# Attention's q, k and v laid out by the host, with fp32 products in place of split fp16 ones

## The chip, the cores and the metric

The program runs on one core of a Trainium2 chip. The metric is device time in microseconds (us) of one execution, lower is better. The figure for the kernel before is the median of three runs; the trace is of one execution more.

## The reference

Three layers follow each other. Attention over B=4 batches, H=8 heads, S=576 tokens and D=64 has a mask that leaves each query at most 32 keys: heads 0 to 3 see the 32 last tokens, heads 4 to 7 every fourth of the 128 last. Its output feeds two mixtures of experts, one with a greedy assignment of 288 tokens to each of 8 experts, one dense with balanced weights.

```python
def _attn_ref(q, k, v):                       # 4, 8, 576, 64
    scores = scale * np.matmul(q, k.transpose(0, 1, 3, 2))
    rel = pos[:, None] - pos[None, :]
    mask_plain = (rel >= 0) & (rel < 32)
    mask_dil = (rel >= 0) & (rel < 32 * 4) & (rel % 4 == 0)
    masks = np.stack([mask_plain if h < H // 2 else mask_dil for h in range(H)], axis=0)
    scores = np.where(masks[None, :, :, :], scores, -1000000000.0)
    scores = scores - np.max(scores, axis=-1, keepdims=True)
    attn = np.exp(scores)
    attn = attn / (np.sum(attn, axis=-1, keepdims=True) + 1e-09)
    return np.matmul(attn, v).astype(np.float32)

def _moe_ref(x, w_gate, w1, w2):              # x 2304 x 512, 8 experts, 1024 hidden
    order = np.argsort(-(x @ w_gate).flatten())
    # in this order each token goes to the first expert that still has room (288 each)
    for e in range(E):
        h = np.maximum(x[assigned == e] @ w1[e], 0.0)
        out[assigned == e] = h @ w2[e]

def _moe2_ref(x, w_gate, w1, w2):             # every expert on every token
    P = np.exp(logits - logits.max())
    for _ in range(8):
        P /= P.sum(1, keepdims=True) + 1e-09
        P /= P.sum(0, keepdims=True) + 1e-09
        P *= N / E
    for e in range(E):
        out += P[:, e:e + 1] * (np.maximum(x @ w1[e], 0.0) @ w2[e])
```

## The kernel before

Products are made of fp16 halves: an fp32 operand a is stored as a high part (fp16 of a) and a low part (fp16 of the rest), and a product is the sum of high·high, high·low and low·high, three matrix products into one accumulator.

**Attention, preparation.** q and k come in with tokens on partitions, in five tiles of 64 or 128 partitions (`TILES`, `load_qk`). Each tile is copied and scaled (`t_copy`: k on VectorE, q on ScalarE), transposed in fp32 on TensorE (`t_group`), and taken out of PSUM as a high part by ScalarE and a low part by VectorE (`t_evac`). `warm` are idle products of zeros.

**Attention, the loop.** A unit is 96 queries of up to eight heads: four of the plain kind (kind 0) and four of the dilated kind (kind 1), whose tokens are taken in residue order so that its window is 32 wide too; kind 1 runs one block ahead. There are NU = 25 units, and only the 128 keys that a block can see take part. Iteration n works on several units at once, in program order on each engine:

```python
scores(n); row_max(n)                  # mask products (L215) and products q·k (L223); L230, L231
p_evac(n - 1, p_trans(n - 1))          # transposes of the probabilities (L247); L255, L256
exps(n)                                # eight exponentials on ScalarE (L239)
pv(n - 2, ...)                         # L269 to L271, and logits of finished tokens
v_split(n + 1); load_v(n + 3)          # L198 on VectorE, L200 and L201 on GpSimd; L118
x_out(n - 3)                           # xo on ScalarE (L288), the rest on GpSimd, store on SyncE (L293)
```

The two heads of a pair lie in opposite halves of the partitions (rows 0 to 63 and 64 to 127), and the products of a pair follow each other on TensorE. The mask is an additive bias: two products of an identity with a table (`mk`, which GpSimd's DMA queue brings) open the accumulation. `x_out` writes a unit's output, as high and low part, to the array `xd` in device memory, from a tile `xo` that comes from a pool of two buffers in units 0 to 17; later units have buffers of their own, in tiles of the preparation that are free by then.

**After attention.** Greedy routing (from the logits) runs on VectorE, GpSimd and TensorE. The experts of the first mixture gather their tokens from `xd` (`gather_x`, L781) and their weights (`fetch_gather`, L772; the weights are fp32 and converted by ScalarE, L751) by indirect DMA on GpSimd's queue. Products of the first mixture are L800, of the second L1064 and L1102; its balancing (L1207) are small fp32 products. `fetched(ph)` starts phase ph's fetches; each `next(w)` issues two weight gathers.

Every engine runs its instructions in program order, and every DMA is issued by the engine that it is written for: SyncE (SP), ScalarE or GpSimd (POOL).

Of the kernel before, what the change touches and what calls it, by code (L numbers as in the profile page):

```python
# [23 lines left out]
QB = 96  # L24
NJ = S // QB
NI = S // 4
SQ = 2.0 ** 7
# [5 lines left out]
SC = 0.125 / (SQ * SQ)  # L33
# [50 lines left out]
TILES = [(0, 64), (64, 128), (192, 128), (320, 128), (448, 128)]  # L84
FILL = {0: 4}
TURN = {NU - 1: (NU - 7, NU - 6), NU: (NU - 5, NU - 4), NU + 2: (NU - 2, NU - 1)}


def attention(tc, q, k, v, masks, wg, ident, xd, L, zero):

    nc = tc.nc
    with ExitStack() as ctx:
# [6 lines left out]
        raw, RP, VR, VS, SS, PP, PT, XT = {}, {}, {}, {}, {}, {}, {}, {}  # L99
        src = {"q": q, "k": k}  # L100
        T = {nm: one.tile([128, 2, 4, B * S], F16, name="t" + nm) for nm in "kq"}

        def load_qk(t, nm):
            f0, n = TILES[t]
            x = raw[t, nm] = ld.tile([128, H, 4, D], F32, name="raw" + nm)
            f = f0
            while f < f0 + n:
                b, i = divmod(f, NI)
                m = min(NI - i, f0 + n - f)
                nc.sync.dma_start(x[f - f0:f - f0 + m].rearrange("i h r d -> i h (r d)"),  # L110
                                  src[nm][b].rearrange("h (i r) d -> i h (r d)", r=4)[i:i + m])
                f += m

        def load_v(u):
            t = VR[u] = vp.tile([128, H, D], F32, name="rawv")
            for kind, (b, j) in UNITS[u].items():
                for p, n, tok, st in tokens_of(max(QB * j - 32, 0), 128, kind):
                    nc.sync.dma_start(t[p:p + n, 4 * kind:4 * kind + 4], bass.AP(  # L118
                        tensor=v.tensor, offset=v.offset + (b * H + 4 * kind) * S * D + tok * D,
                        ap=[[st * D, n], [S * D, 4], [1, D]]))  # L120
# [8 lines left out]
        idh = one.tile([QB, QB], F16)  # L129
        mk = one.tile([QB, MASKS.shape[1], 2, 128], BF)  # L130
# [3 lines left out]
        c128 = one.tile([128, D], F32)  # L134
# [7 lines left out]
        nc.gpsimd.memset(c128, SQ)  # L142
# [6 lines left out]
        def t_copy(t, nm, eng):  # L149
            n = TILES[t][1]  # L150
            x = RP[t, nm] = ld.tile([128, 4, H, D], F32, name="rp" + nm)
            o, i = x[:n], raw.pop((t, nm))[:n].rearrange("i h r d -> i r h d")
            if eng is nc.scalar:
                nc.scalar.activation(o, i, AF.Copy, scale=SQ)
            else:
                nc.vector.tensor_scalar(o, i, SQ, None, op0=OP.mult)

        GC = [0]

        def t_group(t, nm, kind):  # L160
            f0, n = TILES[t]
            x = RP[t, nm]
            tag, bufs = (("ps_s", 2), ("ps_p", 1), ("ps_s", 2))[GC[0] % 3]
            GC[0] += 1
            p = ps.tile([128, 2, 512], F32, name=tag, bufs=bufs)
            for a in range(2):
                for r in range(4):
                    h = 4 * kind + 2 * a
                    nc.tensor.transpose(p[:, a, r * n:(r + 1) * n], x[:n, r, h:h + 2, :], idf[:n, :n])
            return p  # L170

        def t_evac(t, nm, kind, p):
            f0, n = TILES[t]
            pi = p[:, :, :4 * n].rearrange("p a (r i) -> p a r i", r=4)
            if kind == 0:
                parts = [(0, n, [T[nm][:, x, 0:2, 4 * f0:4 * (f0 + n)].rearrange("p a (i r) -> p a r i", r=4)
# [499 lines left out]
class Moe:  # L676
# [540 lines left out]
    def stage1(self, ctx):  # L1217
# [183 lines left out]
```

## Time and profile before

| | |
|---|---|
| median of three runs | 1892.06 us (1890.17 to 1892.47) |
| the profiled execution | 1893.46 us |
| its span (first to last record) | 1891.7 us |
| TensorE busy | 1784.1 us (94% of the span) |
| VectorE busy | 1413.5 us (75%) |
| ScalarE busy | 895.5 us (47%) |
| GpSimd busy | 285.8 us (15%) |

Busy shares are means over stages with different limits: the greater part of the span is the two mixtures of experts, and attention is its start. A stage is read from its own stretch of the span. The profiled execution is 1.40 us above the median.

### The profile page before, as it was taken

How to read it: one execution, taken by the hardware profiler on the slowest of the kernel's cores; microseconds unless marked ns; L12 is line 12 of the kernel's file. 1: busy time of each engine (PE TensorE's matmuls, PEld its weight loads, DVE VectorE, ACT ScalarE, POOL GpSimd, SP SyncE). 2: the span in 40 equal slices, each digit the busy share in tenths (PEclk: the TensorE clock that was granted, in tenths of full speed). 3: DMA queues.
4: the chain of work that ended last, by engine and by line, in shares of the span. 5: the costliest groups of instructions: out<-in, count | busy, mean ns of one | idle time of the engine just before them, and what ended most of it. 6: DMA issues, size and time to landing. Idle time of an engine off the chain costs nothing.

```text
span 1891.7 us, 36726 instructions
## 1 busy us (share of the span) xinstructions
PE 1784.1 (94%) x15082; PEld 1315.0 (70%) x15082; DVE 1413.5 (75%) x2681; ACT 895.5 (47%) x1558; POOL 285.8 (15%) x359
## 2 busy tenths in 40 slices
PE   6898589899999999999999999999999999999998
PEld 4676366666667665677777777777777777777776
DVE  5996687667764477777888788788878878887665
ACT  6885233334334335554555444455544445554333
POOL 0583322223323000000000000000000000000111
PEclk7997699999999999999999999999999999999999
DMA  9275543345445241243533334443333444333120
GB/s 226 66 154 149 113 100 79 108 96 115 115 92 136 73 153 69 82 162 144 193 134 116 141 148 162 154 184 138 120 138 143 162 163 174 141 119 136 75 93 35
DMA packets 139817, 241.21 MB, mean 128 GB/s; under 512 B 74208, under 2 KB 107232, under 8 KB 132736
## 3 DMA queue, kind: packets, MB, share of 16 engines
q1 hardware_dynamic: 118384, 151.25, 24.7%
q0 software_dynamic: 20592, 87.53, 15.6%
q8 instruction: 118, 1.93, 0.4%
q14 instruction: 51, 0.42, 0.1%
q10 hardware_dynamic: 672, 0.08, 0.0%
HBM read 173.74 MB, written 61.74 MB: 124 GB/s over the span
## 4 chain that ended last, share of the span: by engine, by line
PE 58%; issue 10%; DVE 6%; ACT 3%; POOL 1%; DMA 1%; POOLq 0%; ACTq 0%; SPq 0%; DVEq 0%
PE mm L1064 25%; PE mm L1102 22%; PE mm L800 6%; PE mm L881 4%; DVE hl L1021 1%; DMA raw<-in_w2a_dram,widx 1%; POOL out_dram L1116 1%; DVE r L936 1%; ACT raw L933 1%; PE mm L837 1%; DVE w1l L752 1%; ACT acc L1126 0%; PE r L552 0%; DMA lst<-idx 0%; ACT hh L1020 0%
## 5 line engine op out<-in xcount | busy, mean ns | idle before, releaser
L1064 PE MATMUL mm<-xb,w1h 128*128 128x384 f16 x2352 | 575.8, 327 | 5.0 <-DVE mm L1035 4.7
L1102 PE MATMUL mm<-w2h,hh 128*128 128x256 f16 x1764 | 480.8, 273 | 7.5 <-DVE t L1132 4.0
L1102 PE MATMUL mm<-w2h,hl 128*128 128x256 f16 x1764 | 480.8, 273 | 0.0
L1102 PE MATMUL mm<-w2l,hh 128*128 128x256 f16 x1764 | 480.8, 273 | 0.0
L1064 PE MATMUL mm<-xb,w1l 128*128 128x384 f16 x1176 | 384.7, 327 | 0.0
L1102 PEld LDWEIGHTS <-hh 128*128 128x128 f16 x3528 | 345.2, 98 | 51.6 <-issue 9.6
L1064 PEld LDWEIGHTS <-w1h 128*128 128x128 f16 x2352 | 230.7, 98 | 160.1 <-issue 12.7
L1102 PEld LDWEIGHTS <-hl 128*128 128x128 f16 x1764 | 172.6, 98 | 20.0
L1021 DVE TENSOR_TENSOR hl<-r,hh 128x1536 f16<-128x1536 f32 x84 | 147.5, 1756 | 41.3 <-ACT hh L1020 41.3
L1064 PEld LDWEIGHTS <-w1l 128*128 128x128 f16 x1176 | 115.4, 98 | 76.8 <-issue 1.2
L982 POOL DMA_DIRECT2D ws<-raw x48 | 26.0, 541 | 941.6 <-ACT raw L933 674.1
L1016 ACT ACTIVATE r<-mm 128x384 f32<-128x384 f32 x252 | 119.1, 481 | 98.4 <-PE mm L1064 98.3
L1020 ACT ACTIVATE hh<-r 128x1536 f16<-128x1536 f32 x84 | 124.6, 1483 | 46.1 <-DVE r L1045 44.2
L1027 ACT ACTIVATE mm<-mm 128x384 f32<-128x384 f32 x84 | 40.3, 480 | 181.4 <-PE mm L1064 181.4
L1021 DVE TENSOR_TENSOR hl<-S,hh 128x1152 f16<-128x1152 f32 x84 | 113.5, 1351 | 0.0
L800 PE MATMUL mm<-xt,w1h 128*128 128x288 f16 x512 | 97.6, 290 | 6.6 <-ACT xt L814 6.6
L1112 DVE SCALAR_TENSOR_TENSOR acc<-t,P,acc 128x512 f32<-128x512 f32 x126 | 94.7, 752 | 4.5
L803 ACT ACTIVATE w1h<-mm 128x288 f16<-128x288 f32 (+1 forms) x120 | 46.9, 397 | 107.5 <-PE mm L800 98.8
L1020 ACT ACTIVATE hh<-S 128x1152 f16<-128x1152 f32 x84 | 96.3, 1147 | 0.0
L933 ACT ACTIVATE raw<-raw 128x1024 f16<-128x1024 f32 x48 | 50.6, 1055 | 96.3 <-DVE raw L918 50.1
L804 DVE SCALAR_TENSOR_TENSOR w1l<-mm,w1h 128x288 f16<-128x288 f32 (+1 forms) x120 | 50.5, 435 | 57.0 <-ACT w1h L803 56.1
L800 PE MATMUL mm<-x2l,w0h 128*128 128x256 f16 x288 | 80.4, 279 | 9.0 <-DVE x2l L842 7.3
(288 smaller groups left out, 3294.2 us busy)
## 6 DMA issues: line engine op xcount, KB each, us to landing
xb<-xw SPq DMA_DIRECT2D x30, 1344.0 KB
ws<-raw POOLq DMA_DIRECT2D x48, 448.0 KB
ws<-r POOLq DMA_DIRECT2D x48, 448.0 KB
raw<-in_w2b_dram SPq DMA_DIRECT2D x32, 512.0 KB
raw<-in_w1b_dram SPq DMA_DIRECT2D x56, 256.0 KB
w1h<-ws SPq DMA_DIRECT2D x6, 1792.0 KB
w1l<-ws SPq DMA_DIRECT2D x6, 1792.0 KB
w2h<-ws SPq DMA_DIRECT2D x6, 1792.0 KB
```

What stands on the lines that cost most here:

```text
L800: nc.tensor.matmul(p, a[:, k, 128 * f:128 * (f + 1)], rhs(k, b), start=(k == 0 and i == 0), stop=(k == KT - 1 and i == 2))
L803: nc.scalar.activation(h[0][:, f, :n], p, AF.Relu)
L804: nc.vector.scalar_tensor_tensor(h[1][:, f, :n], p, 0.0, h[0][:, f, :n], op0=OP.max, op1=OP.subtract)
L881: nc.tensor.matmul(p, a[:, f, c], b[:, f, :], start=(f == 0 and n == 0), stop=(f == FT - 1 and n == 2))
L933: self.nc.scalar.activation(hi[:, k], x, AF.Copy, scale=sw)
L1016: nc.scalar.activation(o, p, AF.Relu, scale=SH)
L1020: yield nc.scalar.activation(hq[0][:, i, k], x, AF.Copy)
L1021: yield V.tensor_sub(hq[1][:, i, k], x, hq[0][:, i, k])
L1027: nc.scalar.activation(Q[i], P[i], AF.Copy)
L1064: nc.tensor.matmul(p, w[u][:, 2 * j + i // 2, k, 128 * (i % 2):128 * (i % 2 + 1)], x[:, v, r, j], start=(q in (1, 5) and j == 0 and n == 0 ...
L1102: nc.tensor.matmul(p, h[u][:, i, a, 128 * t:128 * (t + 1)], w[v][:, i, b, :], start=(q in (1, 7) and i == 0 and j == 0), stop=(q in (2, 3) ...
L1112: V.scalar_tensor_tensor(self.acc[:, r, :], x, self.P[:, r, e:e + 1], self.acc[:, r, :], op0=OP.mult, op1=OP.add)
```

## The change

The host lays out q and k with the 64 elements of a head on partitions (two heads of a pair one above the other, 128 partitions) and the tokens along the free axis, the dilated kind in residue order; and v as, for each block and kind, the 128 tokens on partitions with a column of 1/256 beside each head's 64. On the chip the preparation goes away: a unit's operands are slices of what was loaded, in fp32. A score takes one fp32 product a head in place of three fp16 ones, and so does the product with v. q and k are loaded in 16 loads (each one batch and kind, 128 partitions of 1152 elements), v in 8 (128 partitions of 1560 elements). Stores to `xd` from units 18 to 24 and the tiles of the turned x have own buffers. In `fetched`, all four weight gathers of the first expert come ahead of its gather of tokens.

```diff
+def lay_qk(a):
+    a = a.reshape(B, 4, 2, S, D).transpose(0, 2, 4, 1, 3).reshape(B, 128, 4, S)
+    r = a[:, :, 2:].reshape(B, 128, 2, NI, 4).swapaxes(3, 4).reshape(B, 128, 2, S)
+    return np.concatenate([a[:, :, :2], r], 2)
+def lay_v(a):
+    out = np.full((B, 2, 128, NJ, 4, D + 1), 1.0 / SX, np.float32)
+    for kind in range(2):
+        for j in range(NJ):
+            for p, n, tok, st in tokens_of(max(QB * j - 32, 0), 128, kind):
+                x = a[:, 4 * kind:4 * kind + 4, tok:tok + st * (n - 1) + 1:st]
+                out[:, kind, p:p + n, j, :, :D] = x.transpose(0, 2, 1, 3)
+    return out
...
+        def load_qk(nm, b, kind):
+            x = raw[nm, b, kind] = one.tile([128, 2, S], F32, name="raw%s%d%d" % (nm, kind, b))
+            nc.sync.dma_start(x, src[nm][b, :, 2 * kind:2 * kind + 2])
+        def load_v(b, kind):
+            x = VR[b, kind] = vp.tile([128, NJ, 4, D + 1], F32, name="rawv%d" % kind, bufs=2)
+            nc.sync.dma_start(x, v[b, kind])
...
-        load_qk(0, "k")
-        nc.scalar.dma_start(idf, ident)
-        load_qk(0, "q")
-        for nm in "kq":
-            load_qk(1, nm)
+        for kind in (1, 0):
+            for nm in "kq":
+                load_qk(nm, 0, kind)
+            if kind:
+                nc.scalar.dma_start(idf, ident)
+        load_v(0, 1)
+        load_v(0, 0)
         nc.gpsimd.dma_start(mk, masks)
...
-        def t_copy(t, nm, eng):
...
-        def t_group(t, nm, kind):
...
-        def t_evac(t, nm, kind, p):
...
-        def v_split(u):
...
             for g in range(gs.start, gs.stop):
-                for n, (x, y) in enumerate(((0, 0), (0, 1), (1, 0))):
-                    for s in range(2):
...
+                for s in range(2):
+                    h = 2 * g + s
+                    b, j = kinds[g // 2]
+                    nc.tensor.matmul(p[:, s, g, :], op_ap("q", h, b, j), op_ap("k", h, b, j), start=False,
+                                     stop=(g + 1 == gs.stop), skip_group_check=True)
...
-            nc.vector.tensor_scalar(nm[:, :, gs], nm[:, :, gs], -SC, None, op0=OP.mult)
+            nc.vector.tensor_mul(nm[:, :, gs], nm[:, :, gs], negc[:, :, gs])
...
-            nc.scalar.activation(th[:, :, gs], pp[:, :, gs], AF.Copy)
-            nc.vector.tensor_sub(tl[:, :, gs], pp[:, :, gs], th[:, :, gs])
-            PT[u] = (th, tl)
+            nc.vector.tensor_copy(t[:, :, gs], pp[:, :, gs])
...
-                nc.tensor.matmul(o, th[x], vh[:, h, :], start=True, stop=False)
-                nc.tensor.matmul(o, tl[x], vh[:, h, :], start=False, stop=False)
-                nc.tensor.matmul(o[:, :D], th[x], vl[:, h, :], start=False, stop=True)
+                b, j = UNITS[u][h // 4]
+                nc.tensor.matmul(o, t[:, h % 2, h // 2, :], VR[b, h // 4][:, j, h % 4, :], start=True, stop=True)
...
-        for t in range(len(TILES)):
...
+        for b in range(1, B if True else 2):
+            for kind in (1, 0):
                 for nm in "kq":
+                    load_qk(nm, b, kind)
+            if b == 1:
+                for kind in (1, 0):
+                    load_v(b, kind)
...
-            if n + 1 < NU:
-                v_split(n + 1)
-            if n + 3 < NU:
-                load_v(n + 3)
+            b, c = divmod(n - NJ - 2, NJ)
+            if 0 <= b < B - 2 and c < 2:
+                load_v(b + 2, 1 - c)
...
             next(w)
-            if ph:
-                next(w)
+            next(w)
             self.gather_x(ph)
-            if not ph:
-                next(w)
```

On TensorE, one unit of the loop before ends with these rows (engine's order, `tq` and `tk` the split q and k, `e` the probabilities, `pth` and `ptl` their transposed high and low part):

```order
L223 MATMUL ps_s<-tk,tq 96x128
L247 MATMUL ps_p<-idf,e 128x96 x8
L269 LDWEIGHTS pth
L269 MATMUL ps_v<-vh,pth 96x65
L270 LDWEIGHTS ptl
L270 MATMUL ps_v<-vh,ptl 96x65
L271 LDWEIGHTS pth
L271 MATMUL ps_v<-vl,pth 96x64
```

After the change a unit stands on TensorE as follows (`rawk`, `rawq` and `rawv` are what was loaded, `pt` the transposed probabilities):

```order
L167 LDWEIGHTS idb
L167 MATMUL ps_s<-mk,idb 96x256
L174 MATMUL ps_s<-rawk_124,rawq_126 96x128 x4
L174 MATMUL ps_s<-rawk_119,rawq_121 96x128 x4
L197 MATMUL ps_p<-idf,e 128x96 x8
L215 MATMUL ps_v<-rawv_130,pt 96x65 x4
L215 MATMUL ps_v<-rawv_128,pt 96x65 x4
```

24 products of scores have become 8, and 24 products with v have become 8; masks and transposes stand where they stood.

On SyncE, the queue that issues loads and stores, loads of v and stores of x alternated before (the first stores of the loop):

```order
L118 DMA rawv<-in_v_dram 128x4x64 [waits DMAHW1_49,DMAHW0_49,DMAHW2_49,DVE_49,Pool_49]
L118 DMA rawv<-in_v_dram 128x4x64
L293 DMA xd<-xo 96x512 [waits Pool_49]
L118 DMA rawv<-in_v_dram 128x4x64 [waits DMAHW4_49,DMAHW5_49,DMAHW3_49,DVE_49]
L118 DMA rawv<-in_v_dram 80x4x64
L118 DMA rawv<-in_v_dram 48x4x64
L293 DMA xd<-xo 96x512 [waits DMAHW6_49,Pool_49]
```

Now the same place, the first stores, reads as follows; the names DMAHW0 to DMAHW7 are eight semaphores that SyncE's DMAs use in turn, so that each DMA waits for the landing of the one eight places before it:

```order
L121 DMA rawk_175<-in_k_dram 128x1152 [waits DMAHW2_49]
L121 DMA rawq_177<-in_q_dram 128x1152 [waits DMAHW3_49]
L121 DMA rawk_179<-in_k_dram 128x1152 [waits DMAHW4_49]
L121 DMA rawq_181<-in_q_dram 128x1152 [waits DMAHW5_49]
L237 DMA xd<-xo 96x512 [waits DMAHW6_49,Pool_49]
L237 DMA xd<-xo 96x512 [waits DMAHW7_49,Pool_49]
L237 DMA xd<-xo 48x512 [waits DMAHW0_49]
```

All 16 loads of q and k and the first four of v are issued ahead of the first store.

On GpSimd, at the start of the first expert, two weight gathers stood before the gather of tokens and two behind it (`raw` are weights, `xg` the tokens, `idx` their numbers):

```order
L772 DMA raw<-in_w1a_dram,widx 128x1024 [waits DMAHW1_49,DVE_49,Activation_49]
L772 DMA raw<-in_w1a_dram,widx 128x1024 [waits DMAHW2_49,Activation_49]
L781 DMA xg<-xd,idx 96x1024 [waits DVE_49]
L781 DMA xg<-xd,idx 96x1024 x2
L772 DMA raw<-in_w1a_dram,widx 128x1024 [waits DMAHW3_49,DMAHW7_49,DMASW0_49,Activation_49]
L772 DMA raw<-in_w1a_dram,widx 128x1024 [waits DMAHW0_49,DMAHW4_49,DMASW1_49,Activation_49]
```

Now all four weight gathers stand ahead of it (the last three of them are shown):

```order
L700 DMA raw<-in_w1a_dram,widx 128x1024 [waits DMAHW6_49,Activation_49]
L700 DMA raw<-in_w1a_dram,widx 128x1024 [waits DMAHW7_49,DMAHW3_49,Activation_49]
L700 DMA raw<-in_w1a_dram,widx 128x1024 [waits DMAHW4_49,DMAHW0_49,Activation_49]
L709 DMA xg<-xd,idx 96x1024 [waits DVE_49]
L709 DMA xg<-xd,idx 96x1024 [waits DMASW0_49]
L709 DMA xg<-xd,idx 96x1024 [waits DMASW1_49]
L700 DMA raw<-in_w2a_dram,widx 128x512 [waits DMASW3_49,DVE_49]
```

The third and fourth weight gather have moved from behind the gather of tokens, which waits for VectorE, to ahead of it.

## Rows read from the trace of the kernel before

**Rows 1.** Busy time by stage: us and (count), mean clock, DMA share, GB/s.

```profile
0.00:58.40 58.40, 39.04 (x198) 27.06 (x199) 36.88 (x45) 39.58 (x33) 2.99 (x10) 0.78 0.79 183
60.60:78.35 17.75, 16.75 (x261) 13.36 (x260) 16.41 (x31) 14.06 (x43) 13.10 (x17) 1.00 0.35 81
78.35:152.40 74.05, 71.77 (x1193) 58.55 (x1191) 68.55 (x134) 60.90 (x180) 63.71 (x73) 1.00 0.64 141
228.40:1891.70 1663.30, 1606.59 (x12908) 1184.28 (x12907) 1244.06 (x2341) 753.15 (x1255) 183.99 (x240) 0.99 0.38 126
```

**Rows 2.** TensorE in order of time: start us, us, engine, line.

```profile
58.42 0.63 PE L215 MATMUL ps_s<-mk,idb 96*96 96x256 bf16 x2
60.59 0.38 PE L215 MATMUL ps_s<-mk,idb 96*96 96x256 bf16 x2
152.39 0.40 PE L215 MATMUL ps_s<-mk,idb 96*96 96x256 bf16 x2
```

**Rows 3.** GpSimd's DMA queue over 0 to 10 us, and over 0 to 11.

```profile
q0 software_dynamic: 165, 0.42, 21.8%
q0 software_dynamic: 208, 0.48, 22.8%
```

**Rows 4.** Busy time again: two stretches of the loads of q and k.

```profile
12.00:20.00 8.00, 5.42 (x27) 3.99 (x28) 4.34 (x4) 2.98 (x4) 0.00 (x0) 0.50 1.11 210
38.00:42.00 4.00, 3.06 (x16) 2.13 (x14) 4.00 (x5) 3.17 (x5) 0.00 (x0) 0.64 1.11 371
```

**Rows 5.** Groups by line, 78.35 to 152.39 us: xcount | busy us, mean ns.

```profile
L230 DVE TENSOR_REDUCE nm<-ps_s 96x8 f32<-96x1024 f32 x18 | 21.8, 1209 | 0.0
L256 DVE TENSOR_TENSOR ptl<-ps_p,pth 128x768 f16<-128x768 f32 x18 | 17.1, 947 | 0.0
L198 DVE TENSOR_SCALAR vh<-rawv 128x512 f16<-128x512 f32 x18 | 13.5, 748 | 0.7 <-DMA rawv<-in_v_dram 0.7
L231 DVE TENSOR_SCALAR nm<-nm 96x8 f32<-96x8 f32 x18 | 3.0, 168 | 0.6
```

**Rows 6.** One unit in order of time.

```profile
78.35 0.62 PE L215 MATMUL ps_s<-mk,idb 96*96 96x256 bf16 x4
78.62 2.15 ACT L239 ACTIVATE e<-ps_s,nm 96x128 f32<-96x128 f32 x8 [0.31 <-DVE nm L231]
78.90 0.87 PE L223 MATMUL ps_s<-tk,tq 64*96 64x128 f16 x24
79.70 1.42 PE L247 MATMUL ps_p<-idf,e 96*128 96x96 f32 x8
80.64 0.65 ACT L288 ACTIVATE xo<-xt 96x512 f16<-96x512 f32 x1
80.96 0.20 PE L269 MATMUL ps_v<-vh,pth 128*96 128x65 f16 x1
81.98 0.21 PE L271 MATMUL ps_v<-vl,pth 128*96 128x64 f16 x1
```

**Rows 7.** An fp32 product of the balancing between fp16 ones, in order of time.

```profile
676.53 0.41 PE L1207 MATMUL r<-P,mean 128*128 128x144 f32 x2
676.78 0.27 PE L800 MATMUL mm<-x2h,w0h 128*128 128x256 f16 x1
```

**Rows 8.** Weight loads of that line: ns min/median/max, first and last start us.

```profile
L1207 PEld LDWEIGHTS r<-P,mean x16: 187/190/192, 676.4 to 729.6; 128*128 128x128 f32 x16
```

**Rows 9.** Weight loads in fp16, the page: xcount | busy us, mean ns.

```profile
L1064 PEld LDWEIGHTS <-w1h 128*128 128x128 f16 x2352 | 230.7, 98 | 160.1 <-issue 12.7
```

**Rows 10.** Start of the first expert, in order of time on each engine.

```profile
206.74 0.92 POOL L781 DMA_INDIRECT xg<-xd,idx  x1 [3.22 <-DVE m L527]
210.74 3.02 POOL L772 DMA_INDIRECT raw<-in_w1a_dram,widx  x1 [0.30 <-issue]
223.93 1.06 ACT L751 ACTIVATE w1h<-raw 128x1024 f16<-128x1024 f32 x1 [14.96 <-DMA raw<-in_w1a_dram,widx]
228.44 0.64 PE L800 MATMUL mm<-xt,w1h 128*128 128x288 f16 x2 [6.58 <-ACT xt L814]
```

More of the change, by code (lines that the diff above doesn't have):

```diff
@@ L26 @@
 NI = S // 4
-SQ = 2.0 ** 7
 SX = 2.0 ** 8
@@ L32 @@
 SG = 2.0 ** 7
-SC = 0.125 / (SQ * SQ)
+SC = 0.125
 def attention_masks():
@@ L97, in attention @@
         ps = ctx.enter_context(tc.tile_pool(name="a_ps", bufs=2, space=bass.MemoryType.PSUM))
-        raw, RP, VR, VS, SS, PP, PT, XT = {}, {}, {}, {}, {}, {}, {}, {}
+        raw, T, VR, SS, PP, PT, XT = {}, {}, {}, {}, {}, {}, {}
         src = {"q": q, "k": k}
[L101 to L120, printed above, removed]
+        def load_qk(nm, b, kind):
[4 more added lines that the diff above has]
+            nc.sync.dma_start(x, v[b, kind])
         def part(u, size):
@@ L129, in attention @@
         idh = one.tile([QB, QB], F16)
+        negc = one.tile([QB, 2, 4], F32)
+        nc.gpsimd.memset(negc, -SC)
         mk = one.tile([QB, MASKS.shape[1], 2, 128], BF)
@@ L160, in t_group @@
-        def t_group(t, nm, kind):
[L161 to L170, printed above, removed]
-        def t_evac(t, nm, kind, p):
[L173 to L176, printed above, removed]
-                                 for x in range(2)])]
-            else:
-                parts, f = [], f0
-                while f < f0 + n:
-                    b, i = divmod(f, NI)
-                    m = min(NI - i, f0 + n - f)
-                    parts.append((f - f0, m, [
-                        T[nm][:, x, 2:4, b * S:(b + 1) * S].rearrange("p a (r i) -> p a r i", r=4)[:, :, :, i:i + m]
-                        for x in range(2)]))
-                    f += m
-            for o, m, (hi, _) in parts:
-                nc.scalar.activation(hi, pi[:, :, :, o:o + m], AF.Copy)
-            for o, m, (hi, lo) in parts:
-                nc.vector.tensor_sub(lo, pi[:, :, :, o:o + m], hi)
@@ L342, in attention @@
         nc.vector.tensor_copy(idh, idf[:QB, :QB])
-        t_copy(0, "k", nc.vector)
-        t_copy(0, "q", nc.scalar)
-        for t in range(len(TILES)):
-            if t + 2 < len(TILES):
+        loaded = []
+        for b in range(1, B if True else 2):
+            for kind in (1, 0):
                 for nm in "kq":
-                    load_qk(t + 2, nm)
-            elif t + 2 == len(TILES):
-                load_v(0)
-                load_v(1)
-                load_v(2)
-            for nm in "kq":
-                for kind in range(2):
-                    t_evac(t, nm, kind, t_group(t, nm, kind))
-                    warm(1)
-                    if t + 1 < len(TILES) and kind == 0:
-                        t_copy(t + 1, nm, nc.vector if nm == "k" else nc.scalar)
-            if t == 0:
-                nc.scalar.activation(wgh, wgf, AF.Copy, scale=SG)
-                nc.vector.scalar_tensor_tensor(wgl, wgf, SG, wgh, op0=OP.mult, op1=OP.subtract)
-        v_split(0)
-        loaded = []
-        store = [ld.tile([128, 4, H, D], F32, name="rp" + nm).bitcast(F16).rearrange("p r h d -> p (r h d)")
-                 for nm in "kkqq"]
-        xl = [t[:, :4 * S].rearrange("p (c q) -> p c q", c=4) for t in store[2:]]
+                    load_qk(nm, b, kind)
+            if b == 1:
+                for kind in (1, 0):
+                    load_v(b, kind)
+        nc.scalar.activation(wgh, wgf, AF.Copy, scale=SG)
+        nc.vector.scalar_tensor_tensor(wgl, wgf, SG, wgh, op0=OP.mult, op1=OP.subtract)
+        xl = [one.tile([128, 4, S], F16, name="xl%d" % kind) for kind in range(2)]
         for n in range(NJ + 1):
-            XO[(B - 1) * NJ + n] = store[n // 4][:QB, 16 * D * (n % 4):16 * D * (n % 4 + 1)].rearrange(
-                "q (k x h d) -> q k x h d", k=2, x=2, h=4)
+            XO[(B - 1) * NJ + n] = one.tile([QB, 2, 2, 4, D], F16, name="xo%d" % n)
         first = S * (B - 1) // 128
```

43 lines of the change are left out of this document (7 added, 36 removed).

## Prediction

> **What bounds the kernel now.** I read the table of busy time by stage first [rows 1]. From 228.40 us to the end (1663 of 1892 us) TensorE is busy 1606.59 us of 1663.30; the change touches nothing there but the order of a few gathers, so I look for its effect ahead of that. Three stretches lie there. Until 58.40 us q and k are loaded and turned: no engine is busy for much more than two thirds of it (ScalarE 39.58 us), TensorE's mean granted clock is 0.78, and the DMAs move 183 GB/s. Then the loop over units: its first five iterations take 17.75 us (3.55 each), the next eighteen 74.05 us (4.11 each). There VectorE has 68.55 us of work, 3.81 a unit; TensorE's 71.77 is no bound, for its records overlap and stretch, as those of a unit show below. Behind the loop stand routing and the start of the first expert. Where each stretch begins is read from the first mask products of iterations 0, 1 and 24 [rows 2]: 58.42, 60.59 and 152.39 us.
>
> **The start.** Loads, copies, 160 transposes and their evacuations go, and the loop can start when its operands have landed. Iteration 0 needs q and k of one kind (two loads of 590 KB), the identity and the masks. Masks come through GpSimd's queue: it moved its last bytes between 10 and 11 us (0.42 MB by 10 us, 0.48 by 11) [rows 3], and nothing in the change moves them forward. With 1 us from landing to use, iteration 0 begins at about 12 us, and iteration 1 follows 2.17 us later as before (60.59 − 58.42), at 14.2. It needs 2.36 MB on SyncE's queue; at the 210 to 371 GB/s that the loads before reach [rows 4] this takes 6.4 to 11.2 us from about 2.4 us on, so it is there by 13.6 at the latest. Gain: 60.59 − 14.2 = **46.4 us**. The bounds: 48 if masks land faster, 42 if both queues slow each other by 4 us. The granted clock was 0.50 from 12 to 20 us before [rows 4], that is 1.2 GHz, and the loop's first iterations may find it there: a tenth of a microsecond in each of five, **+0.5**.
>
> **The stores behind the loads.** SyncE issues all 16 loads of q and k and four of v ahead of the first store of x (the rows of SyncE's order), and `xo` has two buffers, so the third ScalarE copy into it waits until the first store has landed; behind it on ScalarE stand the exponentials, for which everything waits. Ahead of that store lie 16 × 0.59 + 4 × 0.80 + 0.56 MB of masks, identity and gate weights = 13.2 MB. The trace has loads at 371 GB/s (q and k with 128 partitions) and at 210 [rows 4]. The new loads fill 128 partitions, with longer pieces: I take 371, so 35.6 us from 2.4 us, and with 1.5 us for the store 39.5 us. Unstalled, that copy would stand at 80.64 − 60.59 = 20.05 us behind iteration 1, at 34.3. So I set **+5 us**. If the store need not queue behind the loads it is 0; at 210 GB/s the loads last till 65, and the wait is some 32 us, less what later iterations don't lose. That a transfer waits for those issued ahead of it on its queue is not shown by the trace of before, where SyncE mixed loads and stores. The Trainium skill ("DMA: Bandwidth & Descriptors", Queues, rings and completion order) says that descriptors on a ring are consumed in order; by it the wait is real, and no run here shows it yet. It would make the term 5 where the other reading makes it 0.
>
> **The loop's period.** A unit's VectorE operations, each at the mean of its row, add up to the 4.11 us of the period (busy time is 3.81, as records overlap at their edges). Of them the 0.75 us of `vh` goes, the product for the row maximum replaces one of like size, and the copy of `pt` stands for the subtraction of 0.95 [rows 5]: 3.36 are left, so VectorE no longer fills the period, and the chain over engines decides. It goes round once in two periods: masks and scores, row maximum, exponentials, transposes (which TensorE runs an iteration later), the products with v that stand behind them on TensorE, and the next masks but one. Its pieces [rows 6]: the eight exponentials start at 78.62 and end 2.15 later, the transposes stretch over 1.42 us since each waits for its exponential, and the first product with v starts at 80.96, 2.34 us after the first exponential; masks 0.55 (78.35 to 78.90); the 24 products with v 1.02 (80.96 to 81.98), 43 ns each for 65 columns; the scores' 24 products 0.87, 36 ns each for 128 columns, which only goes if products in opposite row halves run beside each other; the row maximum 1.21 and its scale 0.17 [rows 5]. For fp32 the trace has the balancing's products: two with 144 columns take 0.25 us from the first's start to that of the next product (676.53 to 676.78) [rows 7], 125 ns each, while their 187 ns weight loads [rows 8] are partly hidden. Each fp32 product is thus taken as two passes, at 0.87 ns a column 111 ns for 128 columns and 57 for 65. Scores: 16 passes are 1.78 us one after the other, and about 1.0 if halves overlap as in fp16. Products with v: 16 × 57 = 0.91 if weight loads are hidden; an fp32 load costs 90 ns more than an fp16 one (187 against 98) [rows 9], and 16 × 90 = 1.44 if loads set the pace. I take 1.4, as loads of 96 columns take longer than 65 columns of data. Then 2.34 + 1.4 + 0.55 + 1.0 + 1.21 + 0.17, with 0.4 for the hops between engines, are 7.07 us, 3.54 a unit. Logits' products and what chains lose to each other come on top; I take 3.65. ScalarE needs 2.15 + 0.65 = 2.80 [rows 6] and doesn't bind. So 18 × (4.11 − 3.65) = **−8.3 us**; at VectorE's 3.36 it would be −13.5, and with no overlap of halves (0.78 more in a round, period 4.0) −2.0.
>
> Of the weight loads there is a rule that speaks against the change. The fp16 products with v took 1.02 / 24 = 43 ns a pair of load and product [rows 6]. The Trainium skill ("TensorE: Matmul & The Clock Gate", LDWEIGHTS) gives a load P/1.2 ns whatever the columns of data, 80 ns for 96; 24 of them would be 1.9 us, so this trace's fp16 pairs go faster than its rule, and for fp32 no run here shows 96 columns. By it 16 loads are 1.28 us where I have 1.4, and the sum would be 1 us lower.
>
> **Behind the loop.** In the loop's last iterations the subtraction of `ptl` becomes a copy and ScalarE's `pth` goes, half a microsecond off a chain of two units: **−0.5** (0 to −1.5).
>
> **The first expert.** Before, the third and fourth weight gather were issued at 210.74 us, behind the gather of tokens at 206.74, which had waited for VectorE; their data are converted at 223.93, and the first expert's products start at 228.44 [rows 10], when ScalarE had done the conversions and the split of x. With all four ahead, they are issued by about 206, so the data may land 4 us sooner; the token gather comes no earlier, and its data must still be turned and split. I take **−4** (0 to −6).
>
> **Sum.** −46.4 + 0.5 + 5 − 8.3 − 0.5 − 4 = −53.7 us. On the profiled execution's 1893.46 us that is 1839.8; the median of the runs shown is 1.4 below that execution, so 1838 us. What follows, 1663 us of products [rows 1], I leave as it is.
>
> **The rivals.** *The loads are slow, or the stores wait longer.* At 250 GB/s the 13.2 MB last until 55 us and ScalarE waits 22 us rather than 5: −37, 1855 us. For it speaks the first stretch's mean of 183 GB/s [rows 1] with 1 KB pieces, against it 371 with 128 partitions [rows 4]. *fp32 halves don't overlap.* Scores take 1.78 us, the period is 4.0 and the gain of the loop 2: 1844 us. The fp16 scores overlap; nothing here shows it for fp32. *Slower than before:* each of the two passes of an fp32 product waits for a part of its own weight load. TensorE then has 16 × (111 + w) for scores, 16 × (57 + w) for products with v and 0.55 us for masks in a unit, w being what shows of the 187 ns [rows 8]. Apart from period and store wait the change gains 46.4 − 0.5 + 0.5 + 4 = 50.4 us, and 23 iterations took 17.75 + 74.05 = 91.8; so it loses from a period of 142.2 / 23 = 6.2 us on, which is w = 92 ns. At w = 125 the period is 7.24, the loop 166.5, and the kernel takes 24 us more, 1916. Against it: in the balancing a product with its load takes 125 ns in all [rows 7], so at most a small part of the load shows. *The gain is given back:* routing or the weights of the first expert, prefetched during attention, arrive too late for the earlier start. The weight conversion had idle ScalarE before it in [rows 10], 14.96 us, waiting for a gather that is itself tied to routing; a fixed wait of 25 us for weights would leave −28, 1864 us.
>
> **How the numbers follow.** Chances: the forecast with its bounds (1828 to 1848) 0.62; slow loads 0.14; no overlap 0.14, which lies inside those bounds or just above; given back 0.06; slower 0.04. Faster by over 0.2% (some 4 us, what a measurement of this kernel can tell from no change) has 0.95, no change 0.01, slower 0.04. The likeliest time is 1838. The range goes down to 1826 (period 3.36, no wait for stores) and up to 1860, which takes in the greater part of the slow loads and leaves out the given-back and the slower case.
>
> **What would show it.** The first mask products at about 12 and 14 us; ScalarE's third `xo` waiting for a DMA some 5 us near 34 to 40; the loop's period at 3.65 us with VectorE no longer full; iteration 24 at about 103 us; four weight gathers in a row, then tokens, and the expert's products about 4 us nearer to the routing's end. A longer wait of `xo` shows slow loads; scores of 1.8 us a unit show halves one after the other; a gap before the first expert's products that grows by what the loop gained would show it given back, and the forecast wrong.

## The result, and the profile after

The changed kernel takes 1840.45 us (median of 4 runs, 1839.34 to 1841.75) against 1891.12 us for the kernel before on the same chip (4 runs). The ratio is 0.9733, 95% interval 0.9718 to 0.9749: faster by some 50 us. Forecast: 1838, range 1826 to 1860. The profiled execution took 1839.86 us, so against the 1893.46 us of [rows 1] it gains 53.6, where the sum said 53.7. That agreement is better than its parts, as the stages show.

Line numbers have moved: L167 is the mask product (L215 before), L174 the scores, L181 the scale of the row maximum (L231), L189 the exponentials, L197 the transposes, L204 the copy of `pt`, L215 the product with v, L232 and L234 the copy and subtraction of `xo` (L288, L290), L700, L709 and L728 the weight gathers, token gather and expert products (L772, L781, L800).

The changed kernel's busy time by stage answers to [rows 1]; the borders are the first mask products of iterations 0, 1, 6, 7, 9 and 24, the token gather and the first expert's first product. Columns are the stretch and its length, busy time of TensorE, weight loads, VectorE, ScalarE and GpSimd with counts, the granted clock, DMA share and GB/s:

```profile
0.00:12.30 12.30, 6.08 (x18) 2.31 (x19) 1.54 (x15) 1.51 (x2) 2.10 (x8) 0.99 0.86 252
12.30:15.60 3.30, 3.30 (x15) 1.61 (x15) 0.84 (x2) 0.51 (x2) 0.00 (x0) 0.50 1.02 419
15.60:32.69 17.09, 16.98 (x193) 14.55 (x192) 13.16 (x24) 9.94 (x37) 1.81 (x2) 1.00 1.02 413
32.69:36.44 3.75, 3.75 (x46) 3.35 (x46) 3.58 (x7) 2.15 (x8) 0.00 (x0) 1.00 1.02 405
36.44:50.90 14.46, 11.72 (x90) 9.84 (x90) 7.40 (x13) 7.00 (x24) 3.46 (x3) 0.76 0.24 75
50.90:110.59 59.69, 59.69 (x771) 53.39 (x770) 56.33 (x98) 38.87 (x131) 17.31 (x15) 1.00 0.57 141
110.59:162.72 52.13, 37.19 (x433) 23.36 (x429) 35.93 (x114) 20.58 (x39) 7.66 (x8) 0.77 0.45 128
162.72:178.31 15.59, 8.17 (x59) 4.38 (x60) 9.28 (x18) 5.54 (x7) 11.69 (x9) 0.72 0.91 171
178.31:1838.10 1659.79, 1607.07 (x12908) 1184.66 (x12907) 1243.47 (x2338) 753.31 (x1255) 185.50 (x239) 0.99 0.38 126
```

Set against before, stretch by stretch, with the places of [rows 2] and [rows 10]:

| stretch | before, us | after, us | gain | forecast |
|---|---|---|---|---|
| start to iteration 1 | 60.59 | 15.60 | 45.0 | 46.4 |
| iterations 1 to 6 | 17.76 | 17.09 | 0.7 | −0.5 |
| iterations 6 to 24 | 74.04 | 77.90 | −3.9 | +3.3 (8.3 less a wait of 5) |
| iteration 24 to the token gather | 54.35 | 52.13 | 2.2 | 0.5 |
| token gather to first product | 21.70 | 15.59 | 6.1 | 4 |
| the rest | 1663.26 | 1659.79 | 3.5 | 0 |

The loop after iteration 6 became slower, not faster. TensorE in order of time, one undisturbed iteration of the changed kernel (compare [rows 6]):

```profile
25.43 0.60 PE L167 MATMUL ps_s<-mk,idb 96*96 96x256 bf16 x4
25.96 1.12 PE L174 MATMUL ps_s<-rawk,rawq 64*96 64x128 f32 x16
27.01 0.88 PE L197 MATMUL ps_p<-idf,e 96*128 96x96 f32 x8
27.73 1.50 PE L215 MATMUL ps_v<-rawv,pt 128*96 128x65 f32 x16
29.06 0.60 PE L167 MATMUL ps_s<-mk,idb 96*96 96x256 bf16 x4
```

This iteration takes 3.63 us, with TensorE at work throughout: masks 0.53, scores 1.05, transposes 0.72, products with v 1.33. The forecast was 1.0 and 1.4 for the two fp32 parts and 3.65 for the period. It is x16 for 8 heads: two passes each, as assumed. But the period holds in few iterations. ScalarE, changed kernel, in order of time around iteration 7 (in brackets the idle time before, and what ended it):

```profile
32.76 2.15 ACT L189 ACTIVATE e<-ps_s,nm 96x128 f32<-96x128 f32 x8 [1.37 <-DVE nm L181]
39.90 0.63 ACT L232 ACTIVATE xo<-xt 96x512 f16<-96x512 f32 x1 [4.99 <-DMA xd<-xo]
40.44 2.13 ACT L189 ACTIVATE e<-ps_s,nm 96x128 f32<-96x128 f32 x8
```

The third copy of `xo` waits 4.99 us for a store, from 34.9 to 39.9: the forecast had 34.3 to 39.5. From the chain of work that ended last between 25 and 45 us, changed kernel, start and length:

```profile
29.65 10.17 DMA xd<-xo
```

SyncE issued that store at 29.65 us, and it landed 10.17 us later: the transfer was late, not its issue, though SyncE had to wait for an earlier load's landing before it (the semaphores in turn). The iteration takes 8.72 us (36.44 to 45.16), and the next, 45.16 to 50.90, another 5.74 with TensorE at a granted clock of 0.60.

Iterations 9 to 11 take 3.63 to 3.69 us; from iteration 12 on the period is mostly 4.03 us. Three engines of the changed kernel in one such iteration:

```profile
78.35 2.15 ACT L189 ACTIVATE e<-ps_s,nm 96x128 f32<-96x128 f32 x8 [1.37 <-DVE nm L181]
80.36 0.65 ACT L232 ACTIVATE xo<-xt 96x512 f16<-96x512 f32 x1
81.09 1.16 POOL L234 TENSOR_TENSOR xo<-xt,xo 96x512 f16<-96x512 f32 x1 [2.88 <-ACT xo L232]
81.44 0.83 DVE L181 TENSOR_TENSOR nm<-nm,negc 96x8 f32<-96x8 f32 x1
82.38 2.15 ACT L189 ACTIVATE e<-ps_s,nm 96x128 f32<-96x128 f32 x8 [1.37 <-DVE nm L181]
```

VectorE's scale of 8 numbers a row takes 0.83 us in place of 0.16, and ends at 82.27, when GpSimd's subtraction (81.09 + 1.16 = 82.25) ends. The exponentials wait for the scale, the copy for the exponentials, the subtraction for the copy. From one start of the exponentials (78.35) over the copy (80.36), the subtraction (81.09) and its end (82.25) to the next (82.38) it reads as a ring of 4.03 us; the experiments test that.

At the first expert, the changed kernel has all weight gathers issued ahead of the token gather (compare [rows 10]):

```profile
161.04 0.94 POOL L700 DMA_INDIRECT raw<-in_w1a_dram,widx  x1 [0.30 <-issue]
162.72 0.93 POOL L709 DMA_INDIRECT xg<-xd,idx  x1 [0.73 <-DVE m L455]
172.40 1.06 ACT L679 ACTIVATE w1h<-raw 128x1024 f16<-128x1024 f32 x1 [5.60 <-DMA raw<-in_w1a_dram,widx]
177.45 0.81 ACT L742 ACTIVATE xt<-mm 128x768 f16<-128x768 f16 x1 [2.12 <-PE mm L741]
178.31 0.64 PE L728 MATMUL mm<-xt,w1h 128*128 128x288 f16 x2 [0.90 <-ACT xt L742]
```

The last weight conversion comes 9.7 us behind the token gather, where the last two came 17.2 us and later. Before, the split of the tokens (L814), for which the first product waited, stood behind those conversions on ScalarE; now it (L742) waits for the tokens themselves, as TensorE (L741) delivers them.

### The profile page after: what moved, and what is told of

Its sections match the earlier page's. It is cut to its first block, busy times and chain, and to the rows that moved or that the text cites. A ratio compares the mean times of both kernels' runs of the same rounds, so it can differ in the third digit from the quotient of the medians.

```text
span 1838.1 us, 35284 instructions
## 1 busy us (share of the span) xinstructions
PE 1753.9 (95%) x14518; PEld 1297.4 (71%) x14518; DVE 1371.5 (75%) x2625; ACT 839.4 (46%) x1502; POOL 229.5 (12%) x284
## 4 chain that ended last, share of the span: by engine, by line
PE 69%; DVE 11%; issue 10%; DMA 4%; ACT 4%; POOL 2%; SPq 0%; POOLq 0%; DVEq 0%; ACTq 0%
PE mm L992 26%; PE mm L1030 22%; PE mm L728 7%; PE mm L809 5%; PE mm L765 2%; PE ps_v L215 1%; DMA raw<-in_w2a_dram,widx 1%; DVE hl L949 1%; PE r L480 1%; PE ps_p L197 1%; PE ps_s L174 1%; POOL out_dram L1044 1%; DMA rawk<-in_k_dram 1%; DVE G L552 1%; DVE r L864 1%
## 5 line engine op out<-in xcount | busy, mean ns | idle before, releaser
L728 PE MATMUL mm<-xt,w1h 128*128 128x288 f16 x512 | 97.5, 290 | 0.9 <-ACT xt L742 0.9
L728 PE MATMUL mm<-x2l,w0h 128*128 128x256 f16 x288 | 81.0, 281 | 7.4 <-DVE x2l L770 7.4
```

The source lines that it names most:

```text
L728: nc.tensor.matmul(p, a[:, k, 128 * f:128 * (f + 1)], rhs(k, b), start=(k == 0 and i == 0), stop=(k == KT - 1 and i == 2))
```

## The experiments

Ratios are to the kernel before on the same chip; the chips of these runs were up to 0.6% slower than the first, so the stages of the profiles tell more than totals. "6 to 24" is the time from iteration 6's first mask product to iteration 24's; gather is the time from the token gather to the first expert's first product; all in us, each of one profiled execution.

| run | ratio (95%) | it. 1 at | it. 6 at | 6 to 24 | gather |
|---|---|---|---|---|---|
| before | 1 | 60.59 | 78.35 | 74.04 | 21.70 |
| the change | 0.9733 (0.9718 to 0.9749) | 15.60 | 32.69 | 77.90 | 15.59 |
| a_scale | 0.9725 (0.9706 to 0.9744) | 15.38 | 33.41 | 76.36 | 17.36 |
| b_xo4 | 0.9706 (0.9686 to 0.9726) | 15.48 | 33.84 | 72.66 | 16.04 |
| c_nofetch | 0.9749 (0.9730 to 0.9767) | 15.32 | 33.41 | 76.27 | 20.06 |
| d_before_fetch | 0.9975 (0.9962 to 0.9989) | 59.94 | 78.80 | 77.00 | 16.68 |
| e_xofirst | 0.9688 (0.9665 to 0.9710) | 14.67 | 32.53 | 72.89 | 16.33 |
| f_masks | 0.9691 (0.9666 to 0.9716) | 11.93 | 34.62 | 73.28 | 15.77 |
| g_order | one run | 15.09 | 34.44 | 78.67 | 17.35 |
| h_storeq | 0.9720 (0.9684 to 0.9755) | 14.96 | 33.38 | 72.65 | 17.68 |
| i_xomid | 0.9677 (0.9655 to 0.9698) | 15.25 | 32.78 | 69.61 | 15.95 |
| k_start | 0.9721 (0.9699 to 0.9742) | 11.90 | 29.27 | 91.12 | 16.28 |
| j_all | 0.9667 (0.9645 to 0.9689) | 11.58 | 29.80 | 70.23 | 15.88 |

**a_scale.** The product of two tensors back to a scale by a constant:

```diff
-            nc.vector.tensor_mul(nm[:, :, gs], nm[:, :, gs], negc[:, :, gs])
+            nc.vector.tensor_scalar(nm[:, :, gs], nm[:, :, gs], -SC, None, op0=OP.mult)
```

> The changed kernel with the row maximum scaled by a constant again, not by a product of two tensors. Theory (the product of two tensors on VectorE waits for GpSimd's subtraction of xo when the two meet): the 16 scales that took 0.57 to 0.91 us take 0.16 to 0.17, the period of iterations 12 to 24 falls from 4.03 to 3.63 us, 13 x 0.4 = 5 us in all, 1835 us. Rival (the later iterations are longer for the logits' products on TensorE, and the scale is hidden): period stays 4.03, 1840 us.

The theory fell in this form. GpSimd and VectorE of this kernel, in order of time:

```profile
80.24 1.15 POOL L232 TENSOR_TENSOR xo<-xt,xo 96x512 f16<-96x512 f32 x1 [2.89 <-ACT xo L230]
80.58 0.84 DVE L179 TENSOR_SCALAR nm<-nm 96x8 f32<-96x8 f32 x1
```

The scale by a constant is held up as long (0.84 us, ending with the subtraction), and the period is 4.04. So it isn't the kind of operation: either of the two waits when it meets the subtraction. In the kernel before, the same scale took 0.17 us [rows 5]; there it started ahead of that subtraction (78.36 and 78.44 in the iteration of [rows 6]). The rival wasn't shown either: iterations without logits took 4.03 too, as the next run shows.

**b_xo4.** Four buffers of `xo`:

```diff
-                xo = wk.tile([QB, 2, 2, 4, D], F16, name="xo")
+                xo = wk.tile([QB, 2, 2, 4, D], F16, name="xo", bufs=4)
```

> The changed kernel with four buffers of xo in place of two, so that no ScalarE copy waits for the first store. Theory (the wait for the store that stands behind the loads costs its 5 us, and the idle TensorE that it leaves costs 2 us more at the lower clock): iterations 7 and 8 take 3.6 us each in place of 8.7 and 5.7, 7 us in all, 1833 us. Rival (something else is late at the same place, as the values of v or the loads of the next batch): less than 2 us gained, 1839 us.

The wait is gone, and no iteration from 6 on takes more than 4.34 us; iterations 6 to 24 take 72.66 us, 5.2 less. The theory held for the stall, not for its size (7 us were expected, and 3.6 us an iteration): iterations 9 to 11 took 3.63 to 3.69 us in the changed kernel, and iterations 7 to 12 take 4.03 here, so part of what the stall cost comes back as the longer period. Without the stall, then, the loop gained only 74.04 − 72.66 = 1.4 us over before.

**c_nofetch, d_before_fetch.** The order of the gathers undone in the changed kernel, and done alone in the kernel before:

```diff
-            next(w)
-            next(w)
+            next(w)
+            if ph:
+                next(w)
             self.gather_x(ph)
+            if not ph:
+                next(w)
```

> The changed kernel with two weight gathers ahead of the gather of tokens and two behind it, as before. Theory (the 6 us that the first expert gained come from the order of the gathers alone): 6 us slower, 1846 us; the distance from the token gather to the expert's first product is 21 to 22 us again in place of 15.6. Rival (they come from weights that ScalarE finds earlier for another reason): 1840 to 1842 us.

> The kernel before with only the gathers' order changed: all four weight gathers of the first expert ahead of the gather of tokens. Theory: the same 6 us, so 1885 us against 1891, and 15 to 16 us from the token gather to the expert's first product in place of 21.7. Rival (the order helps only with the rest of the change): 1889 to 1892 us.

The distance from token gather to first product goes from 15.6 to 20.1 us when the order is undone, and from 21.7 to 16.7 when it is done in the kernel before (ratio 0.9975, 4.8 us, with an interval just below 1). These two pairs put the order at 4.5 and 5.0 us of the 6.1. But each is a pair of single executions, and the eleven profiles with the new order lie between 15.59 and 17.68; all of them are below the two with the old one (20.06 and 21.70). So the order shortens the stretch, by something between 2.4 and 6.1 us. The total of c_nofetch (0.9749 against 0.9733) has overlapping intervals and doesn't tell by itself.

**e_xofirst.** On top of four buffers, `x_out(n - 3)` ahead of `exps(n)`:

```diff
+            if n >= 3:
+                x_out(n - 3)
             if n < NU:
                 exps(n)
...
-            if n >= 3:
-                x_out(n - 3)
```

> Four buffers of xo, and ScalarE's copy of xo (with GpSimd's subtraction behind it) ahead of the exponentials of its iteration instead of behind them. Theory (the period of 4.03 us is a ring: exponentials 2.0, xo copy 0.7, GpSimd's subtraction 1.2, during which VectorE's small operation on the row maximum doesn't end, then the next exponentials): without the ring the period is TensorE's own 3.63, and 3.63 + 0.31 where logits are made, so iterations 6 to 24 take 66 us in place of 68.9 with four buffers alone. Rival (VectorE's operations in their order, or the chain through PSUM, set 4.03): 68.5 to 69 us.

(The 68.9 us named there were counted from iteration 7; from 6 they are 72.66.) Nothing changed: 72.89 us, the scale at 0.82 to 0.90 in iterations 6 to 24. The edit didn't cut the ring: between two groups of exponentials a copy stands as before, only that of another unit. It tells nothing of the theory; i_xomid does.

**f_masks.** The masks in fp32 on ScalarE's queue, converted by VectorE:

```diff
+                nc.scalar.dma_start(mkf, masks)
...
-        nc.gpsimd.dma_start(mk, masks)
...
+        nc.vector.tensor_copy(mk, mkf)
```

> The changed kernel with the masks loaded in fp32 on ScalarE's queue behind the identity and converted by VectorE, instead of through GpSimd's queue. Theory (masks alone hold the first iteration, at 12.3 us): iteration 0 starts at 8 to 9.5 us, and iteration 1 some 3 us sooner than at 15.6; 3 us gained. Rival (q and k of the second kind, 2.36 MB in all, hold iteration 1, and the masks now take part in the same transfers): iteration 1 not before 14 us, 1 us gained.

Iteration 0 starts at 10.14 us and iteration 1 at 11.93, so masks did hold the start; but iteration 2 only comes at 19.01. ScalarE of this kernel, in order of time:

```profile
16.19 0.23 ACT L297 ACTIVATE wgh<-wgf 128x32 f16<-128x32 f32 x1 [12.75 <-DMA wgf<-in_wg_dram]
17.61 1.13 ACT L190 ACTIVATE e<-ps_s,nm 96x128 f32<-96x128 f32 x4 [1.19 <-DVE nm L182]
```

The gate weights, whose first product in this run (the logits, L281) starts at 67.24 us, are converted ahead of the first exponentials, and now land at 16 us. Iteration 6 is 2 us later than in the changed kernel. But iteration 7, which stands later against the loads' end, takes 4.64 us in place of 8.72, so that iteration 24 comes at 107.90, 2.7 us sooner than with the change alone. The rival, late q and k, isn't what held it: iteration 1 came 3.7 us sooner.

**k_start.** On top of f_masks, that conversion moved to iteration 5:

```diff
-        nc.scalar.activation(wgh, wgf, AF.Copy, scale=SG)
-        nc.vector.scalar_tensor_tensor(wgl, wgf, SG, wgh, op0=OP.mult, op1=OP.subtract)
...
+            if n == 5:
+                nc.scalar.activation(wgh, wgf, AF.Copy, scale=SG)
+                nc.vector.scalar_tensor_tensor(wgl, wgf, SG, wgh, op0=OP.mult, op1=OP.subtract)
```

> Masks on ScalarE's queue in fp32 as in the run before, and the conversion of the gate weights, which stood ahead of the first row maximum on VectorE and the first exponentials on ScalarE, moved to iteration 5. Theory (with early masks the gate weights, which land at 16 us, held everything: the exponentials began at 17.6): the first exponentials start at 12 to 13 us, iteration 1 takes 2 to 4 us in place of 7.1, and iteration 6 starts at 32 to 34 us in place of 38.4. Rival (q and k of the second kind or v land late and hold the loop as long): iteration 6 at 36 us or later.

Iteration 6 starts at 29.27 us, 3.4 sooner than in the changed kernel, and all of it is lost in iteration 7, which now takes 14.41 us. ScalarE's wait, and the two stretches behind iteration 7's start:

```profile
39.07 0.63 ACT L233 ACTIVATE xo<-xt 96x512 f16<-96x512 f32 x1 [7.59 <-DMA xd<-xo]
```

```profile
33.00:47.40 14.40, 5.75 (x47) 5.13 (x46) 7.22 (x10) 4.37 (x15) 2.30 (x2) 0.72 0.38 140
47.40:67.80 20.40, 20.40 (x135) 18.41 (x135) 10.16 (x18) 9.32 (x33) 3.45 (x3) 0.50 0.39 116
```

The first store lands when the loads end, at 39 us, however early the loop starts: the wait grows from 4.99 to 7.59 us. Behind a stretch in which TensorE was busy 5.75 of 14.40 us, the granted clock is 0.50 (1.2 GHz) for three iterations of 6.8 us, though TensorE's records leave no gap in them. In the change itself that price was one iteration of 5.74. Early masks and the late conversion thus helped the start (the 38.4 us named in the expectation is iteration 7's start in f_masks; iteration 6's is 34.62), and the total is no better than the change's. How much of that is the low clock stays open: the profiled execution, 1859.34 us, is 8.6 us longer than any of the other five (1846.57 to 1850.70), which may not have had these three iterations at all.

**g_order.** The scores' products by row half:

```diff
-            for g in range(gs.start, gs.stop):
-                for s in range(2):
+            for s in range(2):
+                for g in range(gs.start, gs.stop):
```

> The changed kernel with the scores' products ordered by row half: four of rows 0 to 63, then four of rows 64 to 127. Theory (fp32 products in opposite halves run beside each other only when they follow each other): the 16 passes of a unit start over 0.85 us in the changed kernel and over 1.6 to 1.8 us here, the period of iterations 3 to 6 grows from 3.63 by 0.8. Rival (the order makes no difference): 0.85 us again.

TensorE of this kernel, in order of time:

```profile
26.14 0.60 PE L167 MATMUL ps_s<-mk,idb 96*96 96x256 bf16 x4
26.68 1.63 PE L174 MATMUL ps_s<-rawk,rawq 64*96 64x128 f32 x16
28.24 0.88 PE L197 MATMUL ps_p<-idf,e 96*128 96x96 f32 x8
30.29 0.60 PE L167 MATMUL ps_s<-mk,idb 96*96 96x256 bf16 x4
```

The scores take 1.56 us (26.68 to 28.24) in place of 1.05, and the period is 4.15 in place of 3.63. So fp32 products in opposite halves do run beside each other, as the fp16 ones did: in the changed kernel the passes start in pairs, the two halves 0.01 us apart and a pair every 0.11 us; grouped, they start one by one every 0.11 us. Grouped, they take 0.5 us more, not the 0.8 expected, for where one half follows the other some four passes (27.2 to 27.5 us) still run in pairs.

**h_storeq.** Stores of units 0 to 2 on GpSimd's queue:

```diff
-                    nc.sync.dma_start(
+                    (nc.gpsimd if u < 3 else nc.sync).dma_start(
```

> The changed kernel with the stores of units 0 to 2 issued on GpSimd's queue instead of SyncE's, two buffers of xo as before. Theory (the first store waits for the loads because it stands behind them on their queue): the store lands within 3 us of its issue, at about 33 us, and the third xo copy waits less than 1 us, 4 to 5 us gained in iteration 7. Rival (the loads fill all DMA engines, and a store waits for them on any queue): the store lands at 38 to 40 us again, and the wait stays at 4 to 5 us.

ScalarE of this kernel, in order of time:

```profile
33.45 2.14 ACT L189 ACTIVATE e<-ps_s,nm 96x128 f32<-96x128 f32 x8 [1.37 <-DVE nm L181]
35.46 0.65 ACT L232 ACTIVATE xo<-xt 96x512 f16<-96x512 f32 x1
```

The third copy waits for nothing, with the loads still running: 0.96 of the DMA engines' time and 386 GB/s between 24 and 38 us. The first store, issued at 29.28 us, landed at 34.50, 5.2 us later (3 were expected) and in time for the copy; in the changed kernel, issued at 29.65, it took 10.17. So its place behind the loads on their queue cost about half of that time; beside the loads on another queue the store, too, took some 5 us. Iterations 6 to 24 take 72.65 us, as with four buffers; the total's interval overlaps that of the change. The Trainium skill ("DMA: Bandwidth & Descriptors", Queues, rings and completion order) says that each DMA engine takes descriptors of one ring in order and goes round between rings; the changed kernel's trace (10.17 us) agrees with the first, this one (5.2 us, with the loads still running) with the second.

**i_xomid.** Four buffers, and the copy in the middle of the next unit's exponentials:

```diff
             for s in range(2):
+                if s and u >= 3:
+                    x_out(u - 3)
                 for g in range(gs.start, gs.stop):
...
-            if n >= 3:
+            if n >= NU:
                 x_out(n - 3)
```

> Four buffers of xo, and ScalarE's xo copy between the fourth and the fifth exponential of a unit, so that GpSimd's subtraction starts 1 us earlier against VectorE's scale of the row maximum. Theory (the ring of exponentials, copy, subtraction, scale makes 4.03 us): the scale takes 0.16 us in every unit, iterations without logits take 3.63 us and those with logits up to 3.95, iterations 6 to 24 take 66 to 69 us in place of 72.7 with four buffers alone and the copy after the exponentials. Rival (TensorE or VectorE's own order sets 4.03): 72 to 73 us again, although the scale takes 0.16.

The same engines of this kernel:

```profile
79.47 0.63 ACT L234 ACTIVATE xo<-xt 96x512 f16<-96x512 f32 x1
80.18 1.15 POOL L236 TENSOR_TENSOR xo<-xt,xo 96x512 f16<-96x512 f32 x1 [2.80 <-ACT xo L234]
81.81 0.16 DVE L181 TENSOR_TENSOR nm<-nm,negc 96x8 f32<-96x8 f32 x1
```

The subtraction ends at 81.33, before the scale begins; the scale takes 0.16 us, still as a product of two tensors. Iterations without logits take 3.63 to 3.87 us but for one of 4.07, those with logits 3.95, and 6 to 24 take 69.61 (66 to 69 were expected), 3.1 less than with four buffers alone. The ring was the bound. What is left is mostly TensorE's own work, by the 3.63 us of its products in an undisturbed iteration and some 0.3 for logits; its busy share can't show that, for in the ring too its records left no gap (59.69 of 59.69 us). The 0.2 us more of some iterations without logits is not explained. The ratio 0.9677 is the lowest of the runs that leave the start alone; its interval overlaps those of b_xo4 and e_xofirst, so it is the stretch that shows the gain.

**j_all.** The edits of i_xomid, f_masks and k_start together:

> All together: four buffers of xo, its copy in the middle of the exponentials, masks on ScalarE's queue, gate weights converted in iteration 5. Theory: iteration 6 starts at 32 to 34 us, iterations 6 to 24 take 66 to 69 us, so the loop ends some 10 us sooner than with the change alone; a ratio to the kernel before of 0.967 or less. Rival (the gains don't add, since the loads' end at about 38 us holds the loop): the ratio of four buffers alone, 0.970.

Iteration 6 starts at 29.80 and 6 to 24 take 70.23, so iteration 24 begins at 100.03 us, 10.6 sooner than in the changed kernel: the gains add once hardly a copy waits for a store (one still does, for 0.72 us at 38.8). The expectation's 32 to 34 and 66 to 69 us fit a count from iteration 7, which starts at 33.45 and is 66.58 us ahead of iteration 24. The ratio, 0.9667 (0.9645 to 0.9689), is below that of the change, 0.9733 (0.9718 to 0.9749), with intervals apart; against i_xomid the two aren't told apart by totals. It beats both kernels.

## Why the prediction was right, and where its parts were not

**The start** was right: 12.30 for 12, held by the masks, which land at 12.26; with masks from another queue it is 10.14 (f_masks). Iteration 1 came at 15.60 for 14.2, because the 3.30 us between run at a granted clock of 0.50 after TensorE had stood still for 5.01 us; in f_masks, j_all and k_start, where it stands still for 2.0 to 2.9 us, the same iteration takes 1.79. The low clock was forecast for the first five iterations; it fell on the first alone.

**The store behind the loads** was right in mechanism, place and length (4.99 for 5), but its loads ran at 252 GB/s until iteration 0 and at 405 to 419 from there to iteration 7, for the 371 taken throughout: that these make up for each other is luck. Taking the wait away is worth 5.2.

**The loop's period is the step that failed**: "Logits' products and what chains lose to each other come on top; I take 3.65", and −8.3 us. Its pieces were good (scores 1.05 for 1.0, products with v 1.33 for 1.4, the copy of `pt` 0.94 for 0.95), but the chain drawn over engines left GpSimd out. With VectorE no longer full, the exponentials, the `xo` copy, GpSimd's subtraction and the scale that it holds up close a ring of 4.03. Without the stall the loop gained 1.4 us, not 8.3; i_xomid, which opens the ring, gains 4.4 over before. "The product for the row maximum replaces one of like size" was wrong only where it met GpSimd: 0.83 us there, 0.16 elsewhere, and the scale by a constant is no better. That a VectorE operation is held up so could be read in the trace of before, VectorE's scale of v and GpSimd's product in two iterations:

```profile
75.44 1.26 POOL L200 TENSOR_TENSOR vsc<-rawv,c 128x512 f32<-128x512 f32 x1
76.78 0.42 DVE L198 TENSOR_SCALAR vh<-rawv 128x512 f16<-128x512 f32 x1
79.60 1.27 POOL L200 TENSOR_TENSOR vsc<-rawv,c 128x512 f32<-128x512 f32 x1
80.40 0.75 DVE L198 TENSOR_SCALAR vh<-rawv 128x512 f16<-128x512 f32 x1
```

Behind GpSimd's product the scale takes 0.42 us, started into it 0.75; the forecast took that 0.75 as VectorE's own work. The logits, taken as small, cost 0.3 us in an iteration once TensorE is the bound.

**The weight loads.** Sixteen passes with v take 1.33 us, 83 ns each: not the 57 of their columns, which fits loads that set the pace, as taken; no run varied the loads to show it. The rule of the Trainium skill ("TensorE: Matmul & The Clock Gate", LDWEIGHTS), 80 ns for 96 columns, comes nearer to this than the 90 of the forecast, and nearer than to the 43 of the fp16 pairs before.

**The first expert**: 6.1 for 4; the order of the gathers is between 2.4 and all of it. **Behind the loop**: 2.2 for 0.5; the stretch takes 51.4 to 52.6 us in all eleven profiles with the change and 54.4 and 55.2 in the two without it; fewer products in the last units and a higher granted clock (0.77 for 0.68) lie in it, and which of them it is was not tried. **The rest** differs by 3.5 us, but lies anywhere from 1660 to 1677 us among profiles whose products there are the same, so it can't be put down to the change.

The loop gave 7.2 us less than forecast and the start 1.4; the other stretches gave 1.2 + 1.7 + 2.1 + 3.5 = 8.5 more. That these cancel is chance; the largest term, 46.4 of 53.7, does not depend on it. Of the rivals, slow loads (405 to 419 GB/s), missing overlap of halves (g_order), weight loads that show for 92 ns (83 − 57 = 26 here) and a gain given back at the first expert (15.59 us for 21.70) are excluded. The lower end of the range, for which period 3.36 and no wait are named, adds up to 1828, not 1826.

## What to carry to other kernels

When an engine stops being the bound, look for rings over the engines that it had hidden, those off the critical path included: here a subtraction on the least busy engine set the period. A load issued early is free only if nothing that a loop waits for stands behind it on its queue; give such stores another queue or more buffers before making the start any faster, or the stall takes the gain back, in one execution here with a low clock on top. And move work that is wanted late out of the way of the first iterations, however small.

## What was not expected of the hardware

A VectorE operation on 96 by 8 numbers, both as product of two tensors and as scale by a constant, lasts until the GpSimd operation that began before it ends: 0.83 and 0.84 us for 0.16. VectorE's reduction from PSUM, which overlapped the same operation, kept its 1.21 us. The Trainium skill ("SBUF — State Buffer", Who interferes with whom) tells of a port pair that both engines share and that the first to start keeps for its whole instruction, for two-input operations and for a scale in its two-port mode; these runs agree with it, though no trace tells in which mode the scale ran. And after the stall of k_start's profiled execution the granted clock stayed at 0.50, that is 1.2 GHz, through 20.4 us in which TensorE's records leave no gap.
